# Where x lies in SBUF against the weights: 128, 160 and 96 bytes modulo 256 in place of 192

## The chip, the core and the metric

The kernel runs on one core of one Trainium2 chip. The metric is the device time of one execution in microseconds; where several runs are given it is their median. Matmuls run on TensorE (PE in the profile), their stationary operands are loaded by LDWEIGHTS (PEld), elementwise work runs on VectorE (DVE) and ScalarE (ACT), and all transfers are issued from SyncE's queue (SP).

## The reference

Attention over pooled keys and values, followed by a two-layer network with softplus, in fp32:

```python
B, H, S, D = 8, 8, 576, 64
k_p = k.reshape(B, H, 72, 8, D).mean(axis=3)
v_p = v.reshape(B, H, 72, 8, D).mean(axis=3)
scores = q @ k_p.transpose(0, 1, 3, 2) / sqrt(D)
attn = softmax(scores)
x = (attn @ v_p).transpose(0, 2, 1, 3).reshape(4608, 512)
h = x @ w_in                                  # 512 -> 2048
g = np.maximum(h, 0.0) + np.log1p(np.exp(-np.abs(h)))
out = g @ w_out                               # 2048 -> 512
```

## The kernel before

The 4608 tokens are worked in 18 chunks of 256 (`CT`). For each chunk the kernel computes the attention and so the chunk's x, transposed: 512 features as 4 blocks of 128 partitions, 256 tokens along the free dimension. To keep fp32 accuracy with one pass per product, x, the weights and g are each kept as a rounded part and a rest ("high" and "low", type fp32r), and every product is the sum of three: high by high, low by high, high by low.

The first product, h = x w_in, has the weights as the stationary operand (128 x 128, loaded anew before each matmul) and x as the moving one (128 x 256). For the first three chunks it is L620 (`ffn1_products`, one block of 128 outputs at a time), from chunk 3 on L668 (`pair1`, two blocks, 24 matmuls in a group). A chunk has 4 x 3 x 16 = 192 such matmuls. The second product has g as the stationary operand and the weights as the moving one: L642 for the first three chunks, L709 for chunk 3, both with 512 columns, and L817 (`pair2_fast`) from chunk 4 on, with 256 columns. There it forms the four blocks of a 2 x 2 product from seven products, so a pair of blocks takes 21 matmuls in place of 24, and a chunk 8 x 21 = 168.

All of TensorE's, ScalarE's, VectorE's and SyncE's work is put in order by a planner (`Order`), which knows for each operation an engine, a cost and what it waits for; its order does not depend on addresses. In the steady part groups of 24 (L668) and of 21 (L817) alternate, and once per chunk come the next chunk's transposes of q (L380), scores (L508), transposes of the probabilities (L461, L561) and attention products (L587, L594).

The addresses come from the order in which tiles are made in the pools, each pool taking the next piece of a partition. Lines 194 to 225 set them so that certain addresses stand in a chosen relation modulo 256 bytes:

- `wl` of group 0 ("w", the weights of 11 of the 16 blocks) begins at 192 modulo 256. It has two halves, first the w_out parts and then the w_in parts; a half is 64 bytes (`ROOM`, 16 words) longer than a multiple of 256, so the w_in parts begin at 0.
- The stage, later group 1 ("l", the last 5 blocks and, from chunk 4 on, the streamed w_in), is laid out the same way: w_out parts at 192, w_in parts at 0.
- A fill of `FILL[1]` = 32 words (128 bytes) follows, then the four x tiles `Xha`, `Xhb`, `Xla`, `Xlb` of 4096 bytes each, all at 192, then a fill of `FILL[2]` = 16 words (64 bytes), so that the next pool begins at 0.
- The g parts (gh, gl, so) begin at 0, and the weights as moving operand of the second product at 192.

So in the first and in the second product the moving operand begins 192 bytes behind the stationary one, modulo 256. `new_x` (L360) chooses the tile for a chunk: chunk 2, the third, takes its own tiles "Sa" and "Sb" with an offset of 48 words (192 bytes), all others one of the two pairs, `Xha`/`Xla` ("a") or `Xhb`/`Xlb` ("b"): chunk 0 "a", chunk 1 "b", chunk 3 "a", chunk 4 "b", and so on in turn. x is written by ScalarE (L601) and VectorE (L604).

Of the kernel before, what the change touches and what calls it, by code (L numbers as in the profile page):

```python
# [10 lines left out]
F32R = mybir.dt.float32r  # L11
# [93 lines left out]
def pooled_attention_softplus_ffn(  # L105
# [14 lines left out]
    P = 128  # L120
# [5 lines left out]
    CT = T * P  # L126
    HP = H // 2
# [13 lines left out]
    xpool = ctx.enter_context(tc.tile_pool(name="xpool", bufs=1))  # L141
    one = ctx.enter_context(tc.tile_pool(name="one", bufs=1))
# [50 lines left out]

    PART, ROOM, LATE = 2 * DM, 16, 5
    BEGINS = [0, FC - LATE, FC]
    FILL = 256 - ROOM, 32, 16, 64
    groups = [None, None]

    def group(f):
        g = 0 if f < FC - LATE else 1  # L200
        n = BEGINS[g + 1] - BEGINS[g]
        if groups[g] is None:
            groups[g] = wpool.tile([P, 2 * (n * PART + ROOM)], F32R, tag="wl"[g], name="wl"[g])
        return groups[g], f - BEGINS[g], n
# [11 lines left out]
    fill = lambda pool, n, i: n and pool.tile([P, n], F32, tag=f"fill{i}", name="fill")  # L216
    fill(wpool, FILL[3], 3)
    group(0)
    fill(wpool, FILL[0] - ROOM, 0)
    stage = wpool.tile([P, 2 * (LATE * PART + ROOM)], I32, tag="l", name="stage")  # L220
    stage_at = lambda i: stage[:, i * 2 * PART:(i + 1) * 2 * PART].rearrange("p (i n) -> p i n", i=2)
    fill(wpool, FILL[1], 1)
    for tag in ("Xha", "Xhb", "Xla", "Xlb"):
        xpool.tile([P, HP, CT], F32R, tag=tag, name="x")
    fill(xpool, FILL[2], 2)
    wi, wo = {}, {}
    t_dram = {(u, i): dram.tile([P, 2, 2, O2], F32, name=f"t{u}_{i}")
# [101 lines left out]
    qt_, x_, e_, pt_, last_ = {}, {}, {}, {}, {}  # L329
# [30 lines left out]
    def new_x(c, name=None):  # L360

        if c == N1 - 1:
            x_[c] = [one.tile([P, HP * CT + 128], F32R, tag=tag, name="x")[:, 48:48 + HP * CT].rearrange(
                "p (m i) -> p m i", m=HP) for tag in ("Sa", "Sb")]
        else:
            name = name or "ab"[c % N1]
            x_[c] = [xpool.tile([P, HP, CT], F32R, tag=tag + name, name="x") for tag in ("Xh", "Xl")]
# [230 lines left out]
    def av_high(c, r, ps, name=None):  # L598
        if c not in x_:
            new_x(c, name)  # L600
        nc.scalar.copy(out=x_[c][0][:, r::2], in_=ps.rearrange("p (g i) -> p g i", g=2))  # L601
# [953 lines left out]
```

## Time and profile before

| what | value |
|---|---|
| median of 3 runs | 888.88 us (888.55 to 888.99) |
| the profiled execution | 888.88 us |
| its span, first to last instruction | 887.2 us |
| granted TensorE clock, mean | 0.997 |
| TensorE busy | 873.3 us, 98% |
| VectorE busy | 646.4 us, 73% |
| ScalarE busy | 416.6 us, 47% |
| HBM | 167.25 MB read, 22.54 MB written |

A matmul is in the profile from its start to the end of its passage through the array, so neighbours overlap, and the sum of their durations exceeds the time that they take. The time that one costs is the interval from its start to the next one's. Rows of the timeline give a group's start in us, its length from the first start to the last end, and the number of instructions in it. In a table of stretches each row has the stretch, its length, and for each engine the busy time with the number of instructions that were under way in it. A row of a group has after the bar its busy time, the mean duration of one in ns, and the idle time before.

### The profile page before, as it was taken

To read this page: it belongs to the slowest core of one execution; us is meant where nothing else is said; L and a number is where in the kernel's file an instruction comes from. 1 tells how busy PE (TensorE), PEld (TensorE's weight loads), DVE (VectorE), ACT (ScalarE), POOL (GpSimd) and SP (SyncE) were. 2 spreads that over 40 slices of the span, in tenths; PEclk is the share of its full clock that TensorE was granted. 3 is DMA by queue.
4 is the path that set the end of the run, shared out by engine and by line. 5 is a ranking of instruction groups with operands and counts; after the bars stand their busy time and mean duration, and the time that the engine had idled before them with its cause. 6 is when DMAs were issued, how large, how long until landed. Compare 5 with 4: busy or idle time off the path is not lost.

```text
span 887.2 us, 20509 instructions
## 1 busy us (share of the span) xinstructions
PE 873.3 (98%) x8280; PEld 830.8 (94%) x8280; DVE 646.4 (73%) x1601; ACT 416.6 (47%) x852; POOL 3.8 (0%) x33
## 2 busy tenths in 40 slices
PE   7999999999999999999999999999999999999997
PEld 4689998899999999999999999999999999999997
DVE  5899999788858788677776566778576565747454
ACT  5954343355353545445444435353545354535432
POOL 1000000000000000000000000000000000000000
PEclk9999999999999999999999999999999999999999
DMA  8966544445887778696877575678656565736472
GB/s 261 321 203 210 170 166 159 163 156 201 288 283 225 234 250 266 207 268 197 279 232 223 190 223 205 191 258 252 215 181 232 183 214 178 251 143 236 170 248 83
DMA packets 107086, 191.12 MB, mean 215 GB/s; under 512 B 46064, under 2 KB 60400, under 8 KB 106992
## 3 DMA queue, kind: packets, MB, share of 16 engines
q1 hardware_dynamic: 106992, 189.82, 65.3%
q8 instruction: 65, 1.06, 0.5%
q14 instruction: 29, 0.24, 0.1%
HBM read 167.25 MB, written 22.54 MB: 214 GB/s over the span
## 4 chain that ended last, share of the span: by engine, by line
PE 95%; DMA 2%; DVE 1%; ACT 1%; issue 0%; SPq 0%; DVEq 0%; ACTq 0%
PE h L668 37%; PE m L817 30%; PE acc L642 8%; PE h L620 7%; PE acc L709 3%; PE avp L587 2%; PE qTp L380 2%; PE ptp L461 2%; PE sc L508 1%; PE avp L594 1%; DMA l<-wi 1%; ACT E L425 1%; DMA kvl<-in_v_dram 1%; PE m L508 0%; PE sc L400 0%; PE ltp L561 0%
## 5 line engine op out<-in xcount | busy, mean ns | idle before, releaser
L668 PE MATMUL h<-x,l 128*128 128x256 f32 x2748 | 338.1, 279 | 1.0 <-DMA l<-wi 1.0
L668 PEld LDWEIGHTS h<-x,l 128*128 128x128 f32 x2748 | 324.0, 188 | 2.6 <-DMA l<-wi 1.4
L676 ACT ACTIVATE g<-h 128x512 f32<-128x512 f32 x120 | 71.8, 598 | 286.0 <-PE h L668 285.9
L817 PE MATMUL m<-w,so 128*128 128x256 f32 x1134 | 148.4, 278 | 0.0
L817 PEld LDWEIGHTS m<-w,so 128*128 128x128 f32 x1134 | 138.3, 188 | 0.1
L727 DVE TENSOR_TENSOR sf<-g 128x128 f32<-128x128 f32 x112 | 32.7, 292 | 136.5 <-ACT g L676 136.4
L741 ACT CAST so<-sf 128x512 fp32r<-128x512 f32 x112 | 69.7, 622 | 63.6 <-DVE sf L730 61.0
L817 PE MATMUL m<-w,gh 128*128 128x256 f32 x476 | 92.0, 282 | 0.0
L746 DVE TENSOR_TENSOR so<-sf,so 128x512 fp32r<-128x512 f32 x112 | 77.3, 690 | 17.9 <-ACT so L741 16.1
L817 PEld LDWEIGHTS m<-w,gh 128*128 128x128 f32 x476 | 72.1, 188 | 0.0
L697 DVE TENSOR_TENSOR gl<-g,gh 128x384 fp32r<-128x384 f32 (+1 forms) x120 | 67.2, 560 | 2.4 <-ACT gh L690 2.4
L817 PE MATMUL m<-w,gl 128*128 128x256 f32 x238 | 66.2, 278 | 0.0
L690 ACT ACTIVATE gh<-h 128x384 fp32r<-128x384 f32 (+1 forms) x120 | 59.3, 494 | 0.0
L625 ACT ACTIVATE g<-h 128x256 fp32r<-128x256 f32 x96 | 32.0, 382 | 55.5 <-PE h L620 33.5
L620 PEld LDWEIGHTS h<-x,w 128*128 128x128 f32 x396 | 48.6, 188 | 2.7 <-ACT g L625 0.6
L620 PE MATMUL h<-x,w 128*128 128x256 f32 x396 | 49.8, 278 | 0.2 <-ACT g L625 0.2
L817 PEld LDWEIGHTS m<-w,gl 128*128 128x128 f32 x238 | 44.9, 189 | 0.0
L838 DVE TENSOR_TENSOR o<-o,m 128x256 f32<-128x256 f32 x98 | 39.7, 418 | 4.0 <-PE m L817 0.9
L642 PE MATMUL acc<-w,g 128*128 128x512 f32 x132 | 41.9, 399 | 0.0
L817 PE MATMUL m<-l,gh 128*128 128x256 f32 x196 | 38.1, 283 | 0.0
L730 DVE TENSOR_TENSOR sf<-g,sf 128x128 f32<-128x128 f32 x112 | 32.7, 292 | 3.9
L431 DVE TENSOR_REDUCE sm<-E 128x8 f32<-128x576 f32 x30 | 21.2, 748 | 18.3 <-ACT E L343 18.3
(210 smaller groups left out, 1261.0 us busy)
## 6 DMA issues: line engine op xcount, KB each, us to landing
l<-wi SPq DMA_DIRECT2D x224, 512.0 KB
out_dram<-o SPq DMA_DIRECT2D x36, 256.0 KB
q<-in_q_dram SPq DMA_DIRECT2D x32, 256.0 KB
kst<-in_k_dram SPq DMA_DIRECT2D x24, 288.0 KB
vst<-in_v_dram SPq DMA_DIRECT2D x24, 256.0 KB
stage<-in_moe_w_in_dram SPq DMA_DIRECT2D x22, 256.0 KB
stage<-in_moe_w_out_dram SPq DMA_DIRECT2D x11, 512.0 KB
wi<-w SPq DMA_DIRECT2D x11, 512.0 KB
```

The lines of the kernel that those rows point to most:

```text
L620: nc.tensor.matmul(out=ps[:, 0:CT], lhsT=row(w, kc), rhs=x[:, kc], start=first and kc == j == 0, stop=last and kc == KC - 1 and j == 2)
L642: nc.tensor.matmul(out=accs[c][t], lhsT=a[:, ts], rhs=w, start=f == 0 and j == 0, stop=f == FC - 1 and j == 2)
L668: nc.tensor.matmul(out=ps[:, k * CT:(k + 1) * CT], lhsT=row(w, kc), rhs=x_[c][i][:, kc], start=first and n == 0, stop=last and n == len(or ...
L676: nc.scalar.activation(out=g, in_=x.rearrange("p (b i) -> p b i", i=P), func=AF.Softplus)
L690: nc.scalar.activation(out=gh, in_=quarters(c, x.rearrange("p (b i) -> p b i", i=P)), func=AF.Softplus)
L697: nc.vector.tensor_tensor(out=gl, in0=quarters(c, g), in1=gh.bitcast(F32), op=ALU.subtract)
L727: tt(out=sf[:, 2], in0=g[:, 0], in1=g[:, 2], op=ALU.add)
L730: tt(out=sf[:, 3], in0=g[:, 3], in1=sf[:, 1], op=ALU.subtract)
L741: nc.scalar.copy(out=so[:, 0], in_=ss[c, u])
L746: nc.vector.tensor_tensor(out=so[:, 1], in0=sf, in1=so[:, 0].bitcast(F32), op=ALU.subtract)
L817: nc.tensor.matmul(out=ms[c][n], lhsT=x, rhs=y, start=u == 0 and j == 0 and n in (1, 6, 5, 4), stop=u == FP - 1 and j == 2 and n in (2, 7, ...
L838: nc.vector.tensor_tensor(out=o, in0=in0, in1=m[n], op=how)
```

## The change

The x tiles get other places. `FILL[1]` becomes 16 words (64 bytes), so that the first x tile begins at 128 modulo 256. The tiles are made in the order `Xha`, `Xla`, `Xhb`, `Xlb`, and a fill of 8 words (32 bytes) behind `Xla` puts the second pair at 160. `FILL[2]` becomes 24 words (96 bytes). The third chunk's x begins 24 words (96 bytes) into its tiles. The w_in parts stay at 0, so these are the offsets of x to the weights in the first product. No instruction is added or removed.

```diff
-    FILL = 256 - ROOM, 32, 16, 64
+    FILL = 256 - ROOM, 16, 24, 64
...
     fill(wpool, FILL[1], 1)
-    for tag in ("Xha", "Xhb", "Xla", "Xlb"):
+
+    for tag in ("Xha", "Xla", "Xhb", "Xlb"):
         xpool.tile([P, HP, CT], F32R, tag=tag, name="x")
+        if tag == "Xla":
+            fill(xpool, 8, 4)
     fill(xpool, FILL[2], 2)
...
         if c == N1 - 1:
-            x_[c] = [one.tile([P, HP * CT + 128], F32R, tag=tag, name="x")[:, 48:48 + HP * CT].rearrange(
+            x_[c] = [one.tile([P, HP * CT + 128], F32R, tag=tag, name="x")[:, 24:24 + HP * CT].rearrange(
                 "p (m i) -> p m i", m=HP) for tag in ("Sa", "Sb")]
```

## The prediction

> **What bounds the kernel now.** I read the page first, for the engine that carries the time, then the waits of TensorE, then single stretches of the timeline, and last a table of stretches.
>
> ```profile
> span 887.2 us, 20509 instructions
> PE 873.3 (98%) x8280; PEld 830.8 (94%) x8280; DVE 646.4 (73%) x1601; ACT 416.6 (47%) x852; POOL 3.8 (0%) x33
> PE 95%; DMA 2%; DVE 1%; ACT 1%; issue 0%; SPq 0%; DVEq 0%; ACTq 0%
> ACT g L676 <- PE h L668: 285.9, 107, 5.0
> PE h L668 <- DMA l<-wi: 1.0, 1, 1.0
> ```
>
> TensorE is busy for 98% of the span and is 95% of the chain that ended last. ScalarE waits 285.9 us for TensorE's first product; TensorE's own longest wait in the steady part is 1.0 us, once, for streamed weights. So the time is the number of matmuls times the interval from one start to the next, and the change, which touches only addresses that matmuls read, can act only on that interval.
>
> The matmuls whose moving operand is x:
>
> ```profile
> L668 PE MATMUL h<-x,l 128*128 128x256 f32 x2748 | 338.1, 279 | 1.0 <-DMA l<-wi 1.0
> L668 PE MATMUL h<-x,w 128*128 128x256 f32 x132 | 16.5, 278 | 0.0
> L620 PE MATMUL h<-x,w 128*128 128x256 f32 x396 | 49.8, 278 | 0.2 <-ACT g L625 0.2
> L620 PE MATMUL h<-x,l 128*128 128x256 f32 x180 | 22.3, 278 | 0.0
> ```
>
> They are 2748 + 132 + 396 + 180 = 3456, which is 18 chunks of 192. The 279 ns of one includes its passage through the array and overlaps the next; the interval is read from the starts of neighbouring groups. Here are the same 24 matmuls of L668 at two places, and eight transposes of L461, whose row among the groups stands first:
>
> ```profile
> L461 PE MATMUL ptp<-ident,pm 128*128 128x128 f32 x144 | 20.0, 273 | 0.2 <-DVE x L604 0.2
> ```
>
> ```profile
> 243.61 2.88 PE L668 MATMUL h<-x,l 128*128 128x256 f32 x24
> 246.33 0.39 PE L817 MATMUL m<-w,gh 128*128 128x256 f32 x2
> ...
> 258.92 1.03 PE L461 MATMUL ptp<-ident,pm 128*128 128x128 f32 x8
> ...
> 290.27 2.99 PE L668 MATMUL h<-x,l 128*128 128x256 f32 x24
> 293.10 0.40 PE L817 MATMUL m<-w,gh 128*128 128x256 f32 x2
> ```
>
> At 243.61 the 24 take 246.33 - 243.61 = 2.72 us, 113.3 ns each. At 290.27 they take 2.83 us, 117.9 ns each. Same line, same shapes, and by the layout the same offset of 192 bytes modulo 256. So there are two rhythms, a quick one of 113.3 and a slow one of 117.8, 4.5 ns apart. They are not an average of scatter; whole stretches keep one of them (the columns are the stretch, its length, TensorE's busy time and number of matmuls, the granted clock, the DMA share and GB/s):
>
> ```profile
> 37.60:38.80 1.20, 1.20 (x12) 1.00 1.13 411
> 281.00:306.00 25.00, 25.00 (x214) 1.00 0.70 222
> 423.00:447.00 24.00, 24.00 (x205) 1.00 0.82 261
> 470.00:494.00 24.00, 24.00 (x206) 1.00 0.63 206
> 563.00:588.00 25.00, 25.00 (x223) 1.00 0.78 244
> 626.90:634.50 7.60, 7.60 (x67) 1.00 0.60 212
> 703.00:727.00 24.00, 24.00 (x205) 1.00 0.63 204
> 745.60:747.80 2.20, 2.20 (x21) 1.00 0.88 281
> 750.00:775.00 25.00, 25.00 (x223) 1.00 0.69 222
> 797.00:820.00 23.00, 23.00 (x205) 1.00 0.64 217
> ```
>
> 205 matmuls take 23.00 us at 797 and 24.00 us at 703 and 423. The clock is 1.00 in all of them, and the DMA share does not sort them (0.63 in a slow stretch, 0.64 and 0.78 in quick ones). A rhythm, once taken, holds through both L668 and L817 until the scores, transposes or attention products of the next chunk interrupt the stream; what follows starts anew:
>
> ```profile
> 280.77 0.29 PE L508 MATMUL m<-kT,qT 64*64 64x72 f32 x3
> 280.98 1.68 PE L668 MATMUL h<-x,l 128*128 128x256 f32 x12
> ...
> 749.06 0.28 PE L508 MATMUL m<-kT,qT 64*64 64x72 f32 x3
> 749.27 2.99 PE L668 MATMUL h<-x,l 128*128 128x256 f32 x24
> ```
>
> After 280.98 the stream settles in the slow rhythm, after 749.27 in the quick one, and both begin with a first product behind the scores. I take the rhythm for a repeating pattern of stalls between the read of the moving operand and the load of the next stationary one, whose pattern depends on how the two addresses stand to each other and on the moment at which the stream restarts. That is a reading; no row here shows an address.
>
> **The change part by part.** It issues the same instructions in the same order, with the same waits and DMAs, on every queue; nothing is moved past anything. The two fills and the new one together take 64 + 32 + 96 bytes in place of 128 + 64, so everything behind the x tiles stays where it was. Only x moves: the pair "a" (chunks 0, 3, 5, ... 17: nine chunks, 9 x 192 = 1728 matmuls) to 128, the pair "b" (chunks 1, 4, 6, ... 16: eight, 1536 matmuls) to 160, chunk 2 (192 matmuls) to 96. The products of L817, where the weights are the moving operand, keep 192. The copies on ScalarE and VectorE that write x lie far from the end of the chain by the wait row above; I put them at nothing, and if their cover were gone it would show as a wait of L668 on L604.
>
> What a slow stretch costs: the four long ones (from 281, 423, 470 and 703) last from the restart to the next transposes, about 25 us each, and lose 1.0 us each by the pair 703/797. That is 4.0 us. The short ones I counted from the single starts: 21 stretches at 117.8, from 10 matmuls at 37.6 us to 19 at 745.6 us, 481 matmuls in all, x 4.5 ns = 2.2 us; the rows at 37.60, 626.90 and 745.60 are three of them (such a row also counts the matmuls that are still under way at its start). All slow stretches together: 6.2 us, over 3456 matmuls with x and, by the code, 14 chunks of 168 = 2352 in L817, so the mean interval is 113.3 + 6200 / 5808 = 114.4 ns.
>
> What the new offsets make of it, term by term:
> First, the long slow stretches all begin with, or run into within one group, a product of x. If the slow pattern of stalls belongs to 192 and no offset other than that holds it, the first group of 24 at 128 or 160 breaks it and the rest of the stretch is quick: -4.0 us.
> Second, of the short stretches about half lie wholly in L817, which the change leaves alone: a quarter to a half of 2.2 us goes, say -0.7 us.
> Third, where x and the weights no longer share an offset, the stream meets a new alignment at each switch between L668 and L817. Each chunk has 8 + 8 switches; over the 14 chunks from chunk 4 on that is 224. Nothing in the trace shows such a switch. Its bounds are nothing and one step between the rhythms, 4.5 ns: 0 to 1.0 us. I take the upper part, +0.7 us, since a switch that the trace does show costs something: the 24 behind the scores at 749.27 last 2.99 us, 0.11 us more than the quick 2.88.
> Fourth, the interval at 128, 160 and 96 itself. The trace has no row of it. The nearest are the two rhythms at 192. The lowest interval of TensorE with a full stationary load before each matmul is that of the transposes: (1.03 - 0.27) us over 7 intervals = 108.6 ns for the eight at 258.92, which move 128 columns, not 256. The bounds are therefore 108.6 and 117.8 ns, and for all 3456 matmuls they are worth 3456 x (108.6 - 113.3) = -16 us and 3456 x (117.8 - 113.3) = +15.6 us. I take 113.3, the value that 4479 of the 5808 matmuls show now (all but 4 x 212, 25 us at 117.8 ns each, and the 481), so 0.
>
> Sum: -4.0 - 0.7 + 0.7 + 0 = -4.0 us. The profiled execution took 888.88 us, 1.7 us more than its span, and it is also the median of the runs, so the forecast is 888.9 - 4.0 = 884.9 us. What comes next: a quicker stream asks for weights 4% sooner in those stretches, at DMA shares of 0.63 to 0.82; the one wait of 1.0 us on the streamed weights could grow by some tenths.
>
> By the Trainium skill ("TensorE: Matmul & The Clock Gate", Back-to-back issue gap) 256 columns alone would take 256 / 2.4 + 2.5 = 109.2 ns, an estimate from that page; the trace shows 113.3 at best, so either rhythm holds something that the rule does not have, and by the rule all x products would be 3456 x (109.2 - 113.3) = 14 us shorter if the new offsets took away whatever is added.
>
> **The rivals.**
> Nothing that can be measured. If the rhythm is set by the moment of the restart alone, addresses do nothing: 888.9, or a new draw of the slow stretches, +-1 us for one more or less. For it: both rhythms occur at one offset, so the offset alone does not decide. Against it: the rhythms hold for 25 us over two lines and change only at interruptions, which a pattern of reads would do and a chance event would not. The Trainium skill states this rival as a rule (the same page, Part 2, on loading the stationary operand): the two operands come through read ports of their own, and loading the next one takes nothing from the running matmul. By that rule the change gives 888.9; the trace, with 113.3 and 117.8 for one instruction at one clock, does not bear out that the interval is set by the columns alone, but it cannot show the ports.
>
> Slower: one of the two main offsets settles in the slow rhythm whenever it is used. Place: the chunks of pair "a". Price: 1728 x 4.5 ns = +7.8 us, less 3.1 us, half of the 6.2, that these chunks lose to the slow rhythm already, less 1.0 us gained in the other chunks: about +4 us, 893. If the slow rhythm is carried from x into the products of L817 of those chunks (seven of 168 matmuls, 1176 x 4.5 ns = 5.3 us), 898. For it: the slow rhythm is stable once entered, and 192 gives the quick one for three matmuls in four, so there is room to lose. It decides as soon as the mean interval of x products rises above today's, 114.4 ns.
>
> Much faster: an offset at which the streams hardly meet brings the interval of x products half way to the transposes' 108.6 ns: 3456 x 2.35 ns = 8.1 us, with the 4.0 above 876.8. For it speaks that a lower interval exists for another shape; against it, that the quick rhythm has one value over the whole run, 113.3 for L668 and (205 in 23.00 us) for L817.
>
> That the edit does not shift x at all is excluded by the sizes of the fills.
>
> **How the numbers follow.** The forecast of about 885 has a chance of 0.42, nothing measurable 0.20, slower 0.27, much faster 0.11. The likeliest case has its own range of 882 to 887 (6.2 us gone and no cost of switches, with the rounding; only half of the long stretches gone). For 8 in 10 the range must take in most of the slower rival and part of the much faster one: 875 to 897. A difference under 0.2%, 1.8 us, can't be told from no change here. Faster by more: 0.42 + 0.11 = 0.53; within: 0.20; slower: 0.27.
>
> **What would show it.** Right: the groups of 24 of L668 take 2.72 us from start to start in every chunk, stretches as at 281, 423, 470 and 703 hold 223 matmuls in 25 us, and L817 outside the restarts is quick. The third term is wrong if the first matmul after each switch is not late. Rival one shows unchanged groups of 2.72 and 2.83 us at other places; the slower rival groups above 2.72 us in all chunks of one pair; the much faster one groups below 2.70. A third interval, neither 113.3 nor 117.8, would make the fourth term wrong, and any growth of the wait on the streamed weights beyond 2 us would make the claim wrong that nothing but the interval counts.

## The result, and the profile after

The changed kernel takes 902.56 us, the median of three runs (902.19 to 902.80), against 888.88 (888.55 to 888.99): 1.0154 of the time before, 95% interval 1.0131 to 1.0177. It is slower by 13.7 us, and above the range of the prediction, which ended at 897. The profiled execution took 902.19 us with a span of 900.5, so 13.3 us more span than before. The granted clock is 0.997 in both.

The page of the kernel after: the span, the engines, and the chain that ended last by engine.

```profile
span 900.5 us, 20509 instructions
PE 887.8 (99%) x8280; PEld 845.4 (94%) x8280; DVE 647.2 (72%) x1601; ACT 416.4 (46%) x852; POOL 3.8 (0%) x33
PE 96%; DVE 1%; ACT 1%; DMA 1%; issue 0%; SPq 0%; DVEq 0%; ACTq 0%
```

TensorE is busy 14.5 us longer with the same 8280 matmuls, and the other engines are where they were. The groups after (three lines were added ahead of them, so L668 is now L671, L817 is L820 and L620 is L623; behind the bar the busy time, the mean of one in ns, the idle time):

```profile
L671 PE MATMUL h<-x,l 128*128 128x256 f32 x2748 | 347.9, 282 | 0.0
L679 ACT ACTIVATE g<-h 128x512 f32<-128x512 f32 x120 | 71.7, 598 | 296.4 <-PE h L671 296.3
L820 PE MATMUL m<-w,so 128*128 128x256 f32 x1134 | 148.5, 278 | 0.0
L623 PE MATMUL h<-x,w 128*128 128x256 f32 x396 | 51.6, 282 | 0.0
```

Both groups that move x went up, L668 from 279 to 282 ns and L620 from 278 to 282, while the second product stands at 278. L671 waits for nothing at all; the 1.0 us for streamed weights is gone. ScalarE waits 10 us longer for the first product. So the loss is neither a wait nor another engine: it is the interval between matmuls, the one thing the change could act on. The timeline after, first a group with x of pair "b" (offset 160), then one with pair "a" (128), each with the row that follows it:

```profile
247.07 2.98 PE L671 MATMUL h<-x,l 128*128 128x256 f32 x24
249.88 0.40 PE L820 MATMUL m<-w,gh 128*128 128x256 f32 x2
...
289.00 3.01 PE L671 MATMUL h<-x,l 128*128 128x256 f32 x24
291.85 0.40 PE L820 MATMUL m<-w,gh 128*128 128x256 f32 x2
```

From start to start 2.81 us at 160, 117.1 ns each, and 2.85 us at 128, 118.8 ns each. The prediction asked for 2.72 everywhere. No long stretch is quick any more. Four of them (the columns are those of the prediction's table of stretches):

```profile
475.50:499.50 24.00, 24.00 (x207) 1.00 0.65 213
569.50:594.50 25.00, 25.00 (x215) 1.00 0.73 234
664.50:689.50 25.00, 25.00 (x215) 1.00 0.66 207
759.50:784.50 25.00, 25.00 (x216) 1.00 0.67 212
```

Before, 25 us held 223 matmuls in a quick stretch; now they hold 215 or 216, still at clock 1.00. Summed over the trace from each matmul's start to the next one's, sorted by the product and by the offset that the layout gives (an x matmul behind which a longer pause or other work comes is counted with the gaps):

| matmuls | before, us (count, mean) | after, us (count, mean) |
|---|---|---|
| x, pair "a" | all x at 192: 387.6 (3388, 114.4 ns) | at 128: 201.3 (1695, 118.8 ns) |
| x, pair "b" | | at 160: 177.5 (1506, 117.9 ns) |
| x, third chunk | | at 96: 22.9 (191, 119.7 ns) |
| second product, 256 columns, at 192 | 265.1 (114.7 ns) | 266.5 (115.4 ns) |
| gaps behind an x matmul | 15.7 | 13.7 |

The x products cost 401.7 - 387.6 = 14.1 us more, the second product 1.4 more, the gaps 2.0 less; with 0.2 less for the 512-column matmuls that is the 13.3 us. The place of the loss is plain. The experiments ask why an offset has a price, whether it is x's own place or its relation to the weights, and whether a better one exists.

### The profile page after: what moved, and what is told of

Its sections match the earlier page's. It is cut to its first block, busy times and chain, and to the rows that moved or that the text cites. A ratio compares the mean times of both kernels' runs of the same rounds, so it can differ in the third digit from the quotient of the medians.

```text
span 900.5 us, 20509 instructions
## 1 busy us (share of the span) xinstructions
PE 887.8 (99%) x8280; PEld 845.4 (94%) x8280; DVE 647.2 (72%) x1601; ACT 416.4 (46%) x852; POOL 3.8 (0%) x33
## 4 chain that ended last, share of the span: by engine, by line
PE 96%; DVE 1%; ACT 1%; DMA 1%; issue 0%; SPq 0%; DVEq 0%; ACTq 0%
PE h L671 38%; PE m L820 30%; PE h L623 7%; PE acc L645 7%; PE acc L712 3%; PE avp L590 2%; PE qTp L383 2%; PE ptp L464 2%; PE sc L511 1%; PE avp L597 1%; ACT E L428 1%; DMA kvl<-in_v_dram 1%; PE m L511 0%; PE sc L403 0%; PE ltp L564 0%; PE kps L1055 0%
## 5 line engine op out<-in xcount | busy, mean ns | idle before, releaser
L671 PE MATMUL h<-x,l 128*128 128x256 f32 x2748 | 347.9, 282 | 0.0
L671 PEld LDWEIGHTS h<-x,l 128*128 128x128 f32 x2748 | 333.4, 188 | 1.2
L820 PE MATMUL m<-w,so 128*128 128x256 f32 x1134 | 148.5, 278 | 0.0
L820 PEld LDWEIGHTS m<-w,so 128*128 128x128 f32 x1134 | 138.4, 188 | 0.1
L820 PE MATMUL m<-w,gh 128*128 128x256 f32 x476 | 93.0, 284 | 0.0
L820 PEld LDWEIGHTS m<-w,gh 128*128 128x128 f32 x476 | 72.4, 189 | 0.0
L820 PE MATMUL m<-w,gl 128*128 128x256 f32 x238 | 66.3, 278 | 0.0
L623 PEld LDWEIGHTS h<-x,w 128*128 128x128 f32 x396 | 50.1, 188 | 2.5 <-ACT g L628 0.4
L623 PE MATMUL h<-x,w 128*128 128x256 f32 x396 | 51.6, 282 | 0.0
L820 PEld LDWEIGHTS m<-w,gl 128*128 128x128 f32 x238 | 44.8, 188 | 0.0
L820 PE MATMUL m<-l,gh 128*128 128x256 f32 x196 | 38.4, 284 | 0.0
```

Of the source, the lines that this page charges most:

```text
L623: nc.tensor.matmul(out=ps[:, 0:CT], lhsT=row(w, kc), rhs=x[:, kc], start=first and kc == j == 0, stop=last and kc == KC - 1 and j == 2)
L671: nc.tensor.matmul(out=ps[:, k * CT:(k + 1) * CT], lhsT=row(w, kc), rhs=x_[c][i][:, kc], start=first and n == 0, stop=last and n == len(or ...
L820: nc.tensor.matmul(out=ms[c][n], lhsT=x, rhs=y, start=u == 0 and j == 0 and n in (1, 6, 5, 4), stop=u == FP - 1 and j == 2 and n in (2, 7, ...
```

## The experiments

Theory A: the interval is set by the place of the moving operand against the stationary one, modulo 256, and 128, 160 and 96 have longer intervals than 192. Rivals: it is x's own place (or the place to which ScalarE and VectorE write x) that counts; or traffic of the other engines and the DMAs; or only the moment of the restart, and the change drew badly.

**The curve, without anything beside it (m1_curve).** A kernel of matmuls alone: groups of 36 with 256 columns, each with its own stationary load, the weights at 0 and x at 0, 16, ... 240, first behind four transposes and then behind twelve matmuls of 512 columns; then some differences again with the weights at 64 and 128.

```python
for o in range(0, 256, 16):
    transposes()
    run("x", 36, 256, o, 0)        # count, columns, offset of x, of the weights
...
for wo in (64, 128):
    for o in (64, 128, 192, 224):
        transposes()
        run("moved", 36, 256, (o + wo) % 256, wo)
```

> This kernel leaves the whole computation out: it issues only matmuls of 256 columns in groups of 36, each with a stationary load of its own, with the moving operand at 0, 16, 32, ... 240 bytes to the stationary one modulo 256; once behind transposes and once behind matmuls of 512 columns; then groups with the stationary operand moved by 64 and by 128 bytes. No DMA and no other engine runs beside them. Theory (the interval hangs on the difference of the two addresses modulo 256, whatever runs beside): 113 to 118 ns at 192, 118 to 119 at 128, 117 to 118 at 160, 119 to 120 at 96, as in the changed kernel, and the same at 128 and 192 when both operands are moved. Rival one (the longer interval comes from what runs beside the matmuls in the whole kernel, the address only changing when they meet): one interval near 109 to 113 ns at all sixteen offsets. Rival two (the place of x by itself counts): the moved groups differ from those with the same difference.

The timeline of this kernel; L35 is a group of 36, L41 the transposes behind it:

```profile
57.61 4.39 PE L35 MATMUL acc<-x,w 128*128 128x256 f32 x36
61.84 0.60 PE L41 MATMUL tp<-ident,raw 128*128 128x128 f32 x4
62.20 4.52 PE L35 MATMUL acc<-x,w 128*128 128x256 f32 x36
66.55 0.60 PE L41 MATMUL tp<-ident,raw 128*128 128x128 f32 x4
...
81.01 4.34 PE L35 MATMUL acc<-x,w 128*128 128x256 f32 x36
85.19 0.60 PE L41 MATMUL tp<-ident,raw 128*128 128x128 f32 x4
```

They are offsets 112, 128 and 192. From the group's start to the transposes: 4.23, 4.35 and 4.18 us. With no DMA, no ScalarE and no VectorE at work, 36 matmuls at 128 take 0.17 us more than at 192. The intervals once a group has settled, in ns:

| offset | 0 | 16 | 32 | 48 | 64 | 80 | 96 | 112 |
|---|---|---|---|---|---|---|---|---|
| behind transposes | 120.0 | 118.7 | 117.8 | 118.4 | 117.7 | 120.1 | 119.9 | 113.3 |
| behind 512 columns | 120.0 | 116.6 | 116.7 | 118.4 | 113.3 | 118.4 | 119.9 | 113.3 |

| offset | 128 | 144 | 160 | 176 | 192 | 208 | 224 | 240 |
|---|---|---|---|---|---|---|---|---|
| behind transposes | 118.7 | 118.6 | 117.4 | 119.3 | 113.3 | 119.2 | 118.2 | 117.2 |
| behind 512 columns | 118.6 | 118.7 | 117.4 | 119.2 | 117.8 | 119.2 | 118.4 | 117.2 |

128, 160 and 96 give 118.7, 117.4 and 119.9: what the kernel after shows (118.8, 117.9, 119.7). Only 64 and 192 have both rhythms, by what runs ahead, and 112 is the third that reaches the quick one. With the weights at 64 or 128, the difference 128 again gives 118.7 and 224 gives 118.3 and 118.4; 64 and 192 both give 113.3 with the weights at 64 and 117.8 with them at 128, one of their two rhythms each time. The traffic is out as a cause: the difference modulo 256 brings the intervals about by itself.

**The weights moved, not x (e3_wi64).** The w_in parts begin at 64 instead of 0, x stays at its 192: the difference is 128.

```diff
-    PART, ROOM, LATE = 2 * DM, 16, 5
+    PART, ROOM, LATE = 2 * DM, 32, 5
...
-    FILL = 256 - ROOM, 32, 16, 64
+    FILL = 256 - ROOM, 0, 16, 64
```

> x stays where it is in the kernel before, at 192 modulo 256; the w_in parts move by 64 bytes, so the difference becomes 128 in all chunks. Theory (difference counts): the products of x at 118 to 119 ns in place of 114.4, 3456 x 4.4 ns = 15 us, with what the second product loses some 16 us: 903 to 907 us. Rival two (the place of x by itself counts): x has not moved, so 888 to 890 us. Rival three (the loss of the changed kernel comes from its mixture of three offsets, with a new alignment in each chunk): one offset throughout, 888 to 892 us.

Measured 902.22 us, 1.0136 of before (1.0117 to 1.0156). Its timeline:

```profile
249.77 3.00 PE L668 MATMUL h<-x,l 128*128 128x256 f32 x24
252.60 0.40 PE L817 MATMUL m<-w,gh 128*128 128x256 f32 x2
```

2.83 us for the group, and over the whole run 118.4 ns for x products and 114.5 for the second. That is a little under the 903 to 907 us that were expected, since the second product lost nothing. Not one address of x has changed, and the loss is nearly that of the changed kernel. x's own place, its writers and a bad draw are out, and so is a loss that comes only from the mixture of three offsets.

**Weights and x moved together (e4_both64, e7_shift64).** If the difference is all, then moving both must cost nothing. In e4_both64 the w_in parts go to 64 and x to 0, while g and the weights of the second product stay.

```diff
-    PART, ROOM, LATE = 2 * DM, 16, 5
+    PART, ROOM, LATE = 2 * DM, 32, 5
...
-    FILL = 256 - ROOM, 32, 16, 64
+    FILL = 256 - ROOM, 16, 0, 64
...
-... name="x")[:, 48:48 + HP * CT]
+... name="x")[:, 64:64 + HP * CT]
```

> The w_in parts and x both move by 64 bytes, so the difference stays 192 and x begins at 0 modulo 256. Theory (difference counts): 888.9 us but for a new draw of the slow stretches, 886 to 892. Rival two (the place of x by itself counts): x is at a place like none before, so the interval differs from 114.4 ns by about as much as at 128, some ns in either direction: 895 us or more, or 880 or less.

It missed, and into the range of the rival by which x's own place counts: 899.07 us, 1.0098 (1.0083 to 1.0113). Its x products take 116.5 ns, a mixture of the two rhythms (of the 114 groups with at least 18 matmuls in one piece from chunk 3 on, 94 end in the slow one, before it was 25):

```profile
246.66 2.99 PE L668 MATMUL h<-x,l 128*128 128x256 f32 x24
249.49 0.40 PE L817 MATMUL m<-w,gh 128*128 128x256 f32 x2
```

What I had overlooked is the switch. When a product of x follows one of the second product, the operands that meet are x or the weights in motion and the other product's stationary load beside them, and those now stand at 128 and 0. By the starts, the interval from the second product into x rose from 114.2 to 118.4 ns, from x into the second from 114.65 to 117.4. The switches alone don't make the loss (155 that can be read, 86 x 4.2 + 69 x 2.75 ns = 0.55 us), but each one can throw the stream into the slow rhythm. The test that leaves the switches alone moves everything by 64 bytes, weights, x, g and what lies behind:

```diff
-    FILL = 256 - ROOM, 32, 16, 64
+    FILL = 256 - ROOM, 32, 16, 80
```

> Weights, x, g and all tiles behind them moved by 64 bytes together, so that every difference between the operands of both products, at the switches too, is that of the kernel before; x begins at 0 modulo 256 as in the run with the w_in parts and x moved alone. Theory (only differences count, and that run lost because the load of the next group's first stationary operand stood at 128 and 0 at the switches): 887 to 892 us, products of x at 114 to 115.3 ns. Rival (x at 0 modulo 256, or the weights at 64, cost by themselves): 897 to 900 us, products of x near 116.5 ns.

889.08 us, 0.9992 (0.9978 to 1.0006), x 114.3 ns, second product 114.2. Its row of the groups:

```profile
L668 PE MATMUL h<-x,l 128*128 128x256 f32 x2748 | 337.0, 278 | 0.0
```

With every difference kept, a move of all places by 64 bytes costs nothing.

**The two halves of the change (e1_a128, e2_b160).** Only pair "a" to 128, or only pair "b" to 160, everything else at 192.

```diff
-    FILL = 256 - ROOM, 32, 16, 64
+    FILL = 256 - ROOM, 16, 16, 64
...
-    for tag in ("Xha", "Xhb", "Xla", "Xlb"):
+    for tag in ("Xha", "Xla", "Xhb", "Xlb"):
         xpool.tile([P, HP, CT], F32R, tag=tag, name="x")
+        if tag == "Xla":
+            fill(xpool, 16, 4)
```

> One part of the change alone: pair a at 128, pair b and the third chunk stay at 192. Theory: the 1728 products of pair a at 118.8 ns, those of pair b at 114.4: 1728 x 4.4 = 7.6 us and about half of the loss in the second product: 896 to 898 us. Rival three (the mixture of offsets costs, whatever they are): as much as the whole change, 900 to 904, or with the products of pair b slower too.

902.55 us, 1.0141 (1.0125 to 1.0158): this half alone costs nearly as much as the whole change, more than the 896 to 898 that I expected and in the range of the rival by which a mixture of offsets costs. e3_wi64, though, lost as much with one offset throughout. x at 128 took 118.7 ns, as it should, (118.7 - 114.4) x 1691 = 7.3 us. Most of the other 5 us lies in what did not move: x at 192 went from 114.4 to 115.6 ns, 2.0 us over 1697, and the second product from 114.7 to 115.75, 2.4 us over 2292. The untouched products fell into their slow rhythm more often: of the longer groups, 22 of 52 of pair "b" end in it (11 before) and 50 of 111 of the second product (31 before). Why, no run shows; in e3_wi64, with all x at 128, it was 9 of 111.

```diff
-    FILL = 256 - ROOM, 32, 16, 64
+    FILL = 256 - ROOM, 24, 16, 64
...
-    for tag in ("Xha", "Xhb", "Xla", "Xlb"):
+    for tag in ("Xhb", "Xlb", "Xha", "Xla"):
         xpool.tile([P, HP, CT], F32R, tag=tag, name="x")
+        if tag == "Xlb":
+            fill(xpool, 8, 4)
```

> Pair b alone at 160, the rest at 192. Theory with the curve (160 gives 117.4 ns): the 1536 products of pair b at 117.4 to 117.9 in place of 114.4, 4.6 to 5.4 us; the others at 192 draw the slow rhythm as often as with pair a alone (115.6 to 115.8), some 5 us more: 898 to 901 us. Without the second part 893 to 895.

894.32 us, 1.0064 (1.0040 to 1.0087). x at 160 took 117.7 ns, x at 192 114.8 and the second product 114.9. Here there is little of the extra loss, and the time is the one expected without it (893 to 895). So the halves come to 12.5 and 5.3 us over the runs of before beside them, together more than the 13.7 of the whole: each offset's own interval adds up, the draws of the rhythm in the rest do not.

**A finer curve (m2_fine).** Matmuls alone again: all offsets in steps of 4 bytes, twelve repeats at 64, 112 and 192, and pairs of stationary operands 64 bytes apart in turn, to see whether the load beside the matmul or its own earlier load counts.

> Again only matmuls, the computation left out. First all offsets from 0 to 252 in steps of 4 bytes, 36 matmuls each behind transposes. Theory (the difference of the addresses modulo 256 sets the interval): the values of the first curve again at its sixteen offsets, 113.3 near 112, 113.3 or 117.8 at 64 and 192, and 117 to 120 nearly everywhere else. Then 64, 112 and 192 six times each with different work before: 64 and 192 settle at 113.3 some times and at 117.8 the others, 112 always at 113.3. Last, pairs of stationary operands 64 bytes apart taken in turn, with x so that either the difference to the matmul's own stationary operand is 192, or the difference to the next one's, which is loaded while the matmul runs. If the load beside it is what counts: x at 192 and 0 in turn gives 118 to 120 ns (128 and 0 to the next load), x at 0 and 192 gives 113.3 or 117.8 (192 and 192 to the next load), 64 and 0 gives 120, 0 and 64 gives 113.3 or 117.8. If the matmul's own stationary operand counts: the other way round for the first two, 113.3 to 117.8 and 118 to 120.

Offsets 108, 112 and 116, each up to the transposes behind it:

```profile
152.45 4.56 PE L35 MATMUL acc<-x,w 128*128 128x256 f32 x36
156.85 0.60 PE L41 MATMUL tp<-ident,raw 128*128 128x128 f32 x4
157.20 4.41 PE L35 MATMUL acc<-x,w 128*128 128x256 f32 x36
161.45 0.60 PE L41 MATMUL tp<-ident,raw 128*128 128x128 f32 x4
161.81 4.64 PE L35 MATMUL acc<-x,w 128*128 128x256 f32 x36
166.29 0.60 PE L41 MATMUL tp<-ident,raw 128*128 128x128 f32 x4
```

4.40, 4.25 and 4.48 us: 112 is a single narrow place, its neighbours 4 bytes off settle at 120.0 and 122.4 ns, and the other 63 offsets lie between 116.6 and 123.6 (64 and 192 were slow here). In the repeats 112 reached 113.3 in 12 of 12, after some ten matmuls at 114 to 121; 192 was slow in 12 of 12 and 64 in 11 of 12. In the last part the stationary operand lies at 0 and at 64 in turn, so that a matmul's difference to its own operand is another one than to the next, whose load runs beside it:

| to its own, in turn | to the next, in turn | interval, ns |
|---|---|---|
| 192, 192 | 128, 0 | 119.0 |
| 0, 128 | 192, 192 | 117.9, irregular |
| 64, 192 | 0, 0 | 120.0, irregular |
| 0, 0 | 192, 64 | 116.8 |

The means go with the next operand: 0 beside the matmul gives the 120.0 of the curve, 0 to its own operand does not, and 192 to its own does not help. But the third goes from 116 to 130 ns within one round, where the curve's group at 0 keeps to 119 to 121, and the second and fourth are not the two rhythms again, so I count this part as a lean and not as settled.

**x at 112 (e5_x112).** If 112 is always quick, x belongs there.

```diff
-    FILL = 256 - ROOM, 32, 16, 64
+    FILL = 256 - ROOM, 8, 40, 64
...
-        xpool.tile([P, HP, CT], F32R, tag=tag, name="x")
+        xpool.tile([P, HP * CT + 64], F32R, tag=tag, name="x")
...
-            x_[c] = [xpool.tile([P, HP, CT], F32R, tag=tag + name, name="x") for tag in ("Xh", "Xl")]
+            x_[c] = [xpool.tile([P, HP * CT + 64], F32R, tag=tag + name, name="x")[:, 4:4 + HP * CT].rearrange(
+                "p (m i) -> p m i", m=HP) for tag in ("Xh", "Xl")]
```

> The kernel before with all x at 112 in place of 192, the second product left at 192. Theory, with the curve (112 settled at 113.3 ns behind transposes and behind wide matmuls, 192 at either): the products of x at 113.4 to 113.8 ns, and the second product mostly quick, because a slow rhythm ends at the next group of x: 6.2 us of slow stretches less 1 us for the restarts gone, 883 to 886 us where the kernel before takes 889. If the rhythm is drawn at random whatever the offset: 886 to 893. If the second product keeps or gets the slow rhythm at each switch: 890 to 900.

A miss: 893.08 us, 1.0040 (1.0025 to 1.0056). The time lies in the last range given, but its reason, a slow second product, did not come.

```profile
251.59 2.96 PE L669 MATMUL h<-x,l 128*128 128x256 f32 x24
254.38 0.40 PE L818 MATMUL m<-w,gh 128*128 128x256 f32 x2
```

2.79 us for a group: it settles anew behind each group of the second product, six to thirteen matmuls mostly at 114 to 121 ns, some up to 130, and then 113, a mean of 116.1. The ten matmuls that the repeats of m2_fine show cost little once in a long run, and a lot every 24. The second product, now behind a stream that ends quick, improved to 114.0.

**Switches without the rest (m3_switch).** Matmuls alone, groups of 24 and 21 in turn, five times, with the places of both products and so of the switches set as in the kernels.

> Only matmuls, the computation left out: groups of 24 and 21 in turn, five times each behind transposes, as the two products follow each other. In nine cases both products stand at 112 to their own stationary operands, and only what the switch sees differs: the last moving operand of the first group stands at d - 224 modulo 256, of the second at d, to the stationary operand that is loaded meanwhile for the other group, d = 0, 32, 64, 96, 112, 128, 160, 192, 224. Then as in the kernel before (all at 192), as with the w_in parts and x moved by 64 (192 in both products, 128 and 0 at the switches), as with x alone at 112, and all at 64. Theory (the rhythm is a state that one matmul at another difference can upset): 113.3 ns throughout at d = 112 once settled, a new settling of up to ten matmuls at 118 to 120 behind some switches for other d; all at 192 keeps one rhythm through all ten groups; the case with 128 and 0 at the switches changes or loses its rhythm at a switch. Rival (a switch is nothing special): every case at 112 stays at 113.3 once settled, and the case moved by 64 is as that at 192.

The timeline: first both products at 112, then all as before, then as in e4_both64; each a group of 24 and the 21 behind it.

```profile
137.18 2.88 PE L53 MATMUL acc<-x,w 128*128 128x256 f32 x24
139.90 2.54 PE L53 MATMUL tp<-x,w 128*128 128x256 f32 x21
...
270.49 2.88 PE L53 MATMUL acc<-x,w 128*128 128x256 f32 x24
273.21 2.54 PE L53 MATMUL tp<-x,w 128*128 128x256 f32 x21
...
296.54 2.99 PE L53 MATMUL acc<-x,w 128*128 128x256 f32 x24
299.37 2.56 PE L53 MATMUL tp<-x,w 128*128 128x256 f32 x21
```

2.72 us for the 24 in the first two, 2.83 in the third. Once settled, all at 112 and all at 192 hold 113.3 ns through every switch, and all at 64 holds 117.8. The places of e4_both64 change the rhythm at each switch: from the second pair of groups on the 24 take 117.7 ns and the 21 take 114.4, a mean of 116.2, where the kernel showed 116.5 and 115.4, a mean of 116.1. The places of e5_x112 give 116.4 for the 24 and 113.7 for the 21, where the kernel showed 116.1 and 114.0. The switches explain both misses. In the eight cases with another d than 112 the 24 settled at 113.3 again within twelve matmuls, but the 21 took 118 to 120 ns to their end, although their own difference was 112. In these eight cases alone the second stationary operand lay 16 bytes off a multiple of 32; the runs do not separate this from the switch ahead of it.

**Both products at 112 (e6_all112).** The weights, x and the third chunk are sliced and filled so that both differences, and those at the switches, are 112.

```diff
-    PART, ROOM, LATE = 2 * DM, 16, 5
+    PART, ROOM, LATE = 2 * DM, 36, 5
...
-    FILL = 256 - ROOM, 32, 16, 64
+    FILL = 48 + ROOM, 48, 40, 40
...
-            groups[g] = wpool.tile([P, 2 * (n * PART + ROOM)], F32R, tag="wl"[g], name="wl"[g])
+            groups[g] = wpool.tile([P, 2 * (n * PART + ROOM) + 8], F32R, tag="wl"[g], name="wl"[g])[:, 4:4 + 2 * (n * PART + ROOM)]
```

(and x as in e5_x112).

> The moving operands of both products at 112 to the stationary ones: x at 112, the w_out parts and the streamed sums at 112 as well, so that no switch between the two products changes the difference. Theory (112 always settles at 113.3 ns after about ten matmuls, and a switch with the same difference doesn't disturb it): both products quick everywhere but for some ten matmuls behind each restart, as many restarts as now: the 6.2 us of slow stretches go, and each of some 70 restarts costs about 10 x 5 ns = 50 ns, of which 192 pays some 15 ns: 884 to 887 us against 889, products of x below 114.2 ns. Rival (the switch itself disturbs, whatever the difference): products of x at 116 ns as with x alone at 112, and the second product as slow: 893 to 900 us.

The total missed by far, 901.55 us, 1.0136 (1.0111 to 1.0161), and yet the intervals came as expected: x 114.0 ns, second product 114.2. Where is the loss? In the table of stretches before, and then of e6_all112:

```profile
40.00:80.00 40.00, 39.19 (x348) 1.00 0.65 206
80.00:130.00 50.00, 50.00 (x327) 1.00 0.55 186
```

```profile
40.00:80.00 40.00, 34.84 (x306) 0.96 0.55 187
80.00:130.00 50.00, 45.31 (x280) 0.97 0.44 155
```

Up to 130 us TensorE stands idle for 4.3 and 4.7 us more, and its clock is granted at 0.96 and 0.97. By the time at which the two kernels reach the same matmul, 17.2 us are lost before 130 us, and from 211 us to the end 4.8 are gained. The group that writes the low parts of the weights, before and then in e6_all112, with the idle time behind the second bar:

```profile
L954 DVE TENSOR_TENSOR w<-stage,w 128x1024 fp32r<-128x1024 f32 x11 | 13.2, 1219 | 0.2 <-ACT w L950 0.2
```

```profile
L955 DVE TENSOR_TENSOR w<-stage,w 128x1024 fp32r<-128x1024 f32 x11 | 13.5, 1225 | 12.6 <-issue 3.9 <-DMA wi<-w 3.1 <-PE h L621 2.8
```

The instruction is as long as before (1225 against 1219 ns) but waits 12.6 us in place of 0.2, among others for the transfer of a block of weights and for matmuls that read one. By the program's instruction order, which the trace does not show (it names what released a wait, not the block), the write of a block had got a wait for the transfer of, and the matmuls with, the block before it. So the loss would be a dependency that my edit of the layout had brought in, not an offset; the next run tests that.

**The same without that wait, and its control (e8_split112, e9_split192).** e6_all112 with the two instructions that write the weights' high and low parts issued in halves, which does away with the added waits; and the kernel before with the halves alone.

```diff
-            nc.scalar.copy(out=hi, in_=g.bitcast(F32))
+            for i in range(hi.shape[1]):
+                nc.scalar.copy(out=hi[:, i], in_=g[:, i].bitcast(F32))
...
-            nc.vector.tensor_tensor(out=lo, in0=g.bitcast(F32), in1=hi.bitcast(F32),
-                                    op=ALU.subtract)
+            for i in range(hi.shape[1]):
+                nc.vector.tensor_tensor(out=lo[:, i], in0=g[:, i].bitcast(F32), in1=hi[:, i].bitcast(F32),
+                                        op=ALU.subtract)
```

> As the run with both products at 112, but the two instructions that write a weight block in the early part (the rounding on ScalarE, the subtraction on VectorE) are each issued in two halves, so that a block's write no longer waits for the transfer and the matmuls of the block before it. Theory: the 17.4 us that the first run lost before 130 us came from these waits, and the steady part keeps its gain of 4.9 us. The halves cost 11 x (2 x 0.69 - 1.22) = 1.8 us of VectorE and some 2 us of ScalarE in a part that partly waits for them: 0 to 3 us. Sum: 884 to 888 us against 889. Rival (the weights at 16 modulo 32 bytes are slow to write or to read in the early part, whatever waits there are): 895 us or more.

> The kernel before with nothing changed but the two instructions in halves, everything at 192: the price of the halves alone. Theory: 0 to 3 us slower than before, 889 to 892, but for a new draw of the slow stretches of +-2 us.

e8_split112: 887.0 us (885.07 to 888.65), 0.9974 of before (0.9964 to 0.9983). e9_split192: 890.91 us, 1.0015 (1.0005 to 1.0024). Groups of e8_split112, then two rows of its timeline:

```profile
L669 PE MATMUL h<-x,l 128*128 128x256 f32 x2748 | 335.5, 277 | 0.0
L957 DVE TENSOR_TENSOR w<-stage,w 128x512 fp32r<-128x512 f32 x22 | 14.0, 687 | 0.0
```

```profile
245.13 2.88 PE L669 MATMUL h<-x,l 128*128 128x256 f32 x24
247.85 0.39 PE L818 MATMUL m<-w,gh 128*128 128x256 f32 x2
```

The waits are gone: at the matmul before 130 us where e6_all112 had lost 17.2 us, this kernel has lost 2.0. The group takes 2.72 us, x products 113.9 ns on the mean, and the kernel is faster than both before and after. With equal instructions, 112 against 192 is 887.0 against 890.9, 3.9 us; against the kernel before, without the halves, it is 2.4. (114.4 - 113.9) x 3388 = 1.7 us are x products and (114.7 - 114.2) x 2292 = 1.1 the second product. The two profiled executions lie 4.7 us apart, and there another 0.8 us are the 384 products with 512 columns, and 1.2 us come before 46 us, where e9_split192 waits 1.7 us for VectorE ahead of the transposes of L473 and e8_split112 does not. With the halves as the base, this is about the gain that the prediction hoped for at 128 and 160.

## Why the prediction was wrong

What bounds the kernel held, and so did the claim that only the interval counts: TensorE is 96% of the chain, nothing new waits, and the loss sums up from intervals.

The step that failed is the fourth term, "the interval at 128, 160 and 96 itself", which took 113.3 ns, "so 0". It is 118.8, 117.9 and 119.7 ns. Against the x products of before, slow stretches included, that costs 14.1 us, nearly the whole loss; in the term's own measure, against 113.3 ns, it is 1728 x 5.5 + 1536 x 4.6 + 192 x 6.4 ns = 17.8 us in place of 0. The prediction had named this sign of being wrong, a third interval. I chose the value that most matmuls showed, but every row of it came from one offset, 192, and said nothing of others. The upper bound too was taken from that offset: 117.8 is exceeded at 128 and at 96, in the kernel and in matmuls alone. With that bound, +15.6 us in place of 0, the sum would have been 884.9 + 15.6 = 900.5; the range ended at 897 because the slower rival let only one of the two main offsets be slow.

The first term, -4.0 for the long slow stretches, did not come about: x no longer has a quick rhythm to go back to. The second, -0.7 for the short stretches, had the wrong sign: the second product went up by 1.4 us, from 114.7 to 115.4 ns, and e1_a128 shows the same disturbance stronger. The third, +0.7 for the switches, has no trace of its own: after the change the interval from the second product into x is 114.8 ns and from x into the second product 117.6 (from 128) and 116.2 (from 160), so a switch takes no longer than an interval of the stream that it leaves. The switches' real cost, which the term had not foreseen, is that they can make the next group settle anew (e4_both64, e5_x112). The gaps, which no term had, became 2.0 us shorter. That the forecast missed by 17.7 us, just the fourth term, is luck: the errors of the rest cancel.

The rivals. "Nothing that can be measured" is refuted by e3_wi64, where only the weights moved and 12 us came up. The rule cited with it, from the Trainium skill ("TensorE: Matmul & The Clock Gate", Part 2), that loading the next stationary operand takes nothing from the running matmul, provides for no effect of the operands' places. These runs show one: 118.7 ns at 128 and 113.3 at 112 for one and the same instruction, with nothing else at work. Whether it is the load that takes something they do not show, since no run leaves the loads out. "Slower" had the right sign and the right kind of mechanism, an offset that settles slow; it was too small, as both offsets settle slow, and their intervals are ones of their own and not 192's slow rhythm. "Much faster" is out: nothing in the curve lies below 113.3.

Open remains what in the chip makes the difference modulo 256 count. That the reads of the moving operand and the loads collide fits the curve and the lean in m2_fine, but it is argued, not shown. Nor do the runs show which restart leads to which rhythm at 192.

## What to carry to other kernels

In a kernel like this one, bound by fp32r matmuls of 256 columns with a load before each, the relation of the two operands' addresses is a tuning parameter worth up to 6% of the interval at multiples of 16 bytes (113.3 against 120.1 ns), and here the trace taken at one relation did not tell the price of another: measure the curve first, with matmuls alone, and at the group lengths and switches of the kernel. Where two products alternate, choose the places for the pairs at the switches too. And when a layout edit slows the kernel, look for waits that it brought in before blaming the addresses (e6_all112 lost 17 us before 130 us, of which e8_split112 took back 15).

## What the runs showed of the hardware that was not expected

With fp32r matmuls of 256 columns, one load of 128 x 128 before each, and nothing else running: only the difference 112 modulo 256 settled at 113.3 ns every time (12 of 12 in a row); 64 and 192 have two stable rhythms, 113.3 and 117.8; other multiples of 16 bytes gave 116.6 to 120.1, and offsets 4 bytes beside 112 gave 120.0 and 122.4. With the stationary operand at 0, 64 or 128 the differences 128 and 224 gave the same interval within 0.4 ns; with it 16 bytes off a multiple of 32, and a switch at another difference ahead, the interval was 118 to 120 ns at the difference of 112 too. And the quick rhythm at 112 took some ten matmuls to settle after most restarts, so that it pays in long streams and not in groups of 24 between others at another difference.
